# A fused attention and squared-ReLU kernel: the opening is laid out by other costs, three chunks of the first expanded weights go by DMA, and s is applied at the eviction

## The chip, the cores and the metric

The kernel runs on one core of a Trainium2 chip. The metric is the device time of one execution in microseconds (us). The text calls TensorE PE, VectorE DVE, ScalarE ACT, GpSimd POOL and SyncE SP, as the profile does. SP only issues DMAs here.

## What is computed

There are B = 4 batches of N = 12480 rows x of C = 128 columns, m = 32 inducing rows, and d_ff = 2048. Everything is float32.

```python
scale = 1.0 / np.sqrt(C)
def mab(q, kv):
    s = scale * (q @ kv.transpose(0, 2, 1))
    s = s - s.max(-1, keepdims=True)
    a = np.exp(s)
    a /= a.sum(-1, keepdims=True) + 1e-09
    return a @ kv
h = mab(I, x)
attn = mab(x, h)
...
h = attn @ w_in
r = np.maximum(h, 0.0)
g = s * (r * r) + b
return g @ w_out
```

The weights w_in, w_out and the scalars s and b are float64 in DRAM; the kernel narrows the weights to float32 itself.

## The kernel before

A batch has 26 blocks of 480 rows. Before the first block of a batch, all its rows attend to the inducing rows, which gives h (32 x 128), kept transposed as `hT`. Then `attend` gives the weights of each row on the 32 rows of h (`a2t`, transposed, with high and low halves so that fp32r products keep float32 precision). The second `@ h` and `@ w_in` are one product: `wst` holds h @ w_in (32 x 2048), four times below one another as high and low halves. So a block needs eight *pairs* (`pair`): two matmuls mm1 (L1002, 128x480 each) into a PSUM tile h, a ReLU r (L1014 on ACT or L1016 on DVE), the square's high half (L1080, ACT), the low half (L1045 on DVE, then L1056 on POOL or DVE, or by a DMA that adds), and six matmuls by `w_hi` and `w_lo` (L1112, `out_part`) into one of two PSUM banks x. The bank leaves with the bias by L1125 and a DMA. Work on the next blocks and the next batch stands between the pairs. 4 x 26 x 8 = 832 pairs make the steady stage.

The first batch has no batch ahead of it to hide in: this is the **opening**. The first batch's x comes in 13 tiles of 960 rows (480 KB; x0 to x12). Each tile is scored against the inducing rows (`first_scores`, L568, groups of one or two tiles), and its transposed copy is made by PE and a copy (`turn_x`, L542, L284) or loaded by DMA (`load_first`, L515). The eight chunks of float64 weights (512 KB each: i0 to i3 of w_in, o0 to o3 of w_out) are narrowed (`narrow`, L427 to L445): two masks on DVE, two ACT steps, two DVE steps, and one product on POOL (or DVE). A chunk of w_out is then split into `w_hi` (ACT, L455) and `w_lo` (DVE, L457), both scaled by s; `w_neg` (L464) is two pieces of -w_hi. When the last tile, x0, is scored, the maxima and sums are joined (`h_unit`, `h_sums`, `h_out`: L617 to L690) to `hT`. `attend_first` (L903 to L942) makes the first block's a2t alone; `w_unit` (L703 to L707) makes the four chunks of wst. Then pair 0 can begin.

The order on each engine isn't that of the code. A planner (`Plan.run`) takes units of work with a cost in us, an engine or a choice of them, events that they wait for, and an urgency; it picks what can start soonest, shifted by urgency times a weight, and writes the instructions in that order. `LOCK` marks a DVE step that the planner doesn't place beside a POOL step. `Rules` are its weights, one set for the opening and one for every 32 pairs. Its times only set the order: on the chip each engine runs its list in order, and each instruction waits for what it needs.

```python
yield "ACT", 0.6, ("w_out", c)
nc.scalar.mul(w_hi[:, sl, :], raw[:, sl, :], s_sb)
yield "DVE", 0.63, LOCK
nc.vector.scalar_tensor_tensor(
    out=w_lo[:, sl, :], in0=raw[:, sl, :], scalar=s_sb, in1=w_hi[:, sl, :].bitcast(F32),
    op0=ALU.mult, op1=ALU.subtract,
)
```

In the profile buffer numbers are left out: g stands for g, g1 (raw weights, high halves of squares) and g2, x for the two PSUM banks, h for the PSUM tiles, s for several small tiles. wst is the name of the expanded weights and, in the opening, of the narrowed w_out.

## Time and profile before

| | before |
|---|---|
| median of 3 runs | 1520.68 us (1519.18 to 1521.63) |
| the profiled execution's own time | 1518.01 us |
| its span, first to last instruction | 1516.2 us |
| busy: PE, DVE, ACT, POOL | 99%, 95%, 97%, 95% |
| PE's granted clock | 0.999 |
| first ReLU of pair 0 begins | 53.73 us |
| last eviction ends, last instruction | 1511.93 us, 1516.2 us |

The profile is of one execution. Times are from the start of its span. Most work of PE is in L1112 and L1002; their matmuls overlap, so that a mean of 367 ns for one stands beside a start every 0.20 us. A row of the timeline gives start, duration, engine, line, operation, output and inputs, and in brackets how long the engine had been idle and what ended that.

### The profile page before, as it was taken

The numbers are of one execution on the slowest core, as the hardware profiler recorded it, in microseconds if no ns is written. First come the engines' busy times: TensorE is split into PE (matmuls) and PEld (weight loads), VectorE is DVE, ScalarE is ACT, GpSimd is POOL, SyncE is SP. The second block draws the span as 40 slices with busy tenths as digits, with TensorE's granted clock in tenths as the row PEclk, the third lists the DMA queues.
The fourth block names the chain that finished last, engine by engine and source line by source line (L and its number), as shares of the span: only waits on it lengthen the run. The fifth ranks groups of instructions, "written<-read, shape, count | busy, mean of one in ns | idle before, by whom it ended". The sixth has DMA issues, their size and how long they took to land.

```text
span 1516.2 us, 25236 instructions
## 1 busy us (share of the span) xinstructions
PE 1495.3 (99%) x8215; PEld 1294.9 (85%) x8215; DVE 1435.3 (95%) x1587; ACT 1465.4 (97%) x1767; POOL 1443.7 (95%) x725
## 2 busy tenths in 40 slices
PE   7899999999999999999999999999999999999998
PEld 5588888888888888888898888888889888888887
DVE  5899999999999999999999999999999999999998
ACT  6899999999999999999999999999999999999997
POOL 2599999999999999999999999999999999999998
PEclk9999999999999999999999999999999999999999
DMA  9244545534454454453455534544533334234332
GB/s 342 65 124 128 140 104 158 143 76 125 104 150 127 114 149 105 135 142 83 127 133 137 144 104 118 163 112 105 120 102 93 79 91 112 56 85 108 91 72 53
DMA packets 73810, 178.91 MB, mean 118 GB/s; under 512 B 13520, under 2 KB 40144, under 8 KB 73680
## 3 DMA queue, kind: packets, MB, share of 16 engines
q1 hardware_dynamic: 59280, 128.51, 27.2%
q0 software_dynamic: 14256, 48.67, 17.3%
q8 instruction: 67, 1.10, 0.3%
q14 instruction: 63, 0.52, 0.1%
q10 hardware_dynamic: 144, 0.12, 0.0%
HBM read 74.56 MB, written 25.56 MB: 66 GB/s over the span
## 4 chain that ended last, share of the span: by engine, by line
PE 69%; ACT 4%; issue 3%; POOL 3%; DVE 2%; DVEq 0%; ACTq 0%; POOLq 0%
PE x L1112 48%; PE h L1002 17%; POOL g L1056 3%; ACT r L1014 2%; ACT g L1080 2%; PE x L853 1%; DVE g L1045 1%; PE x L802 1%; PE x L762 1%; DVE h L1045 0%; DVE r L1016 0%; DVE gm L1027 0%; PE x L717 0%; ACT ob L1125 0%; POOL hm L1032 0%
## 5 line engine op out<-in xcount | busy, mean ns | idle before, releaser
L1056 POOL TENSOR_TENSOR g<-g,g 128x960 fp32r<-128x960 f32 x611 | 1399.2, 2665 | 21.7 <-DVE g L1045 13.4
L1112 PE MATMUL x<-g,w_hi 128*128 128x480 f32 x2932 | 920.1, 367 | 1.5 <-POOL g L1056 1.0
L1080 ACT ACTIVATE g<-r 128x960 fp32r<-128x960 f32 x733 | 713.4, 1008 | 12.0 <-PE x L1112 0.9
L1045 DVE SCALAR_TENSOR_TENSOR g<-h,r 128x960 f32<-128x960 f32 x611 | 688.5, 1146 | 24.2 <-ACT r L1014 13.7
L1014 ACT ACTIVATE r<-h 128x960 f32<-128x960 f32 x648 | 608.6, 970 | 12.5 <-PE h L1002 10.2
L1112 PEld LDWEIGHTS x<-g,w_hi 128*128 128x128 f32 x2932 | 550.8, 189 | 52.5 <-issue 6.3
L1112 PE MATMUL x<-g,w_lo 128*128 128x480 f32 x1466 | 537.4, 367 | 1.4 <-ACT g L1080 1.1
L1002 PE MATMUL h<-a2t,wst 128*128 128x480 f32 x1664 | 485.4, 374 | 3.7 <-DVE g L1045 3.2
L1002 PEld LDWEIGHTS h<-a2t,wst 128*128 128x128 f32 x1664 | 299.2, 189 | 82.2 <-issue 33.1
L1112 PEld LDWEIGHTS x<-g,w_lo 128*128 128x128 f32 x1466 | 277.0, 189 | 24.5 <-issue 2.6
L1016 DVE TENSOR_SCALAR r<-h 128x960 f32<-128x960 f32 x184 | 210.8, 1148 | 5.0 <-PE h L1002 3.8
L1056 DVE TENSOR_TENSOR g<-h,g 128x960 fp32r<-128x960 f32 x122 | 140.7, 1153 | 7.8 <-ACT g L1080 1.2
L1045 DVE SCALAR_TENSOR_TENSOR h<-h,r 128x960 f32<-128x960 f32 x122 | 141.0, 1155 | 0.9 <-ACT r L1014 0.8
L1027 DVE SCALAR_TENSOR_TENSOR gm<-h,r 128x960 f32<-128x960 f32 x99 | 113.3, 1145 | 4.3 <-ACT r L1014 4.1
L1032 POOL DMA_DIRECT2D hm<-gm x99 | 113.7, 1148 | 0.1
L1080 ACT ACTIVATE hm<-r 128x960 fp32r<-128x960 f32 x99 | 99.7, 1007 | 0.7
L1112 PE MATMUL x<-hm,w_lo 128*128 128x480 f32 x198 | 72.8, 368 | 0.0
L1112 PE MATMUL x<-hm,w_hi 128*128 128x480 f32 x198 | 72.5, 366 | 0.0
L1125 ACT ACTIVATE ob<-x,bias 128x480 f32<-128x480 f32 x101 | 66.8, 661 | 1.1 <-PE x L1112 0.5
L1112 PE MATMUL x<-hm,w_neg 128*128 128x480 f32 x198 | 56.3, 366 | 0.0
L1112 PEld LDWEIGHTS x<-hm,w_lo 128*128 128x128 f32 x198 | 37.4, 189 | 3.5 <-DVE hl L891 0.8
L1112 PEld LDWEIGHTS x<-hm,w_neg 128*128 128x128 f32 x198 | 37.4, 189 | 2.7
(152 smaller groups left out, 559.4 us busy)
## 6 DMA issues: line engine op xcount, KB each, us to landing
hm<-gm POOLq DMA_DIRECT2D x99, 480.0 KB, 5.3
xt<-in_xT_dram SPq DMA_DIRECT2D x96, 480.0 KB, 5.2
a2t<-hl SPq DMA_DIRECT2D x412, 60.0 KB, 2.0
out_dram<-ob SPq DMA_DIRECT2D x103, 240.0 KB, 2.1
xn<-in_xN_dram SPq DMA_DIRECT2D x18, 512.0 KB, 4.3
xn<-in_xN_dram SPq DMA_DIRECT2D x18, 448.0 KB, 4.8
wst<-whl SPq DMA_DIRECT2D x48, 64.0 KB, 2.0
g<-in_w_in_dram SPq DMA_DIRECT2D x4, 512.0 KB, 10.3
```

Source lines behind the costliest of these rows:

```text
L762: nc.tensor.matmul(ps[M * q:M * (q + 1), 0:BLK], ind_sb, xt[:, q % SB], start=True, stop=True)
L802: nc.tensor.matmul(ps[M * c:M * (c + 1), 0:P], eT[0:rows, n], xn_tiles[b, g, half][0][0:rows, n - half * TH], start=n < P // M, stop=n + P ...
L1002: nc.tensor.matmul(h[:, u, 0:BLK], wst[:, n * P:(n + 1) * P], by_turns(A), start=True, stop=True)
L1014: nc.scalar.activation(out=r, in_=hv, func=AF.Relu)
L1016: nc.vector.tensor_scalar(out=r, in0=hv, scalar1=0.0, scalar2=None, op0=ALU.max)
L1027: nc.vector.scalar_tensor_tensor(out=gm, in0=hv, scalar=-1.0, in1=r, op0=ALU.mult, op1=ALU.mult)
L1032: nc.gpsimd.dma_start(out=hi["t"].bitcast(F32).rearrange("p u t -> p (u t)"), in_=gm.rearrange("p u t -> p (u t)"), accum_op=ALU.add,)
L1045: nc.vector.scalar_tensor_tensor(out=g, in0=hv, scalar=0.0, in1=r, op0=ALU.max, op1=ALU.mult)
L1056: eng.tensor_tensor(out=g2, in0=g, in1=hi["t"].bitcast(F32), op=ALU.subtract)
L1080: nc.scalar.activation(out=hi["t"], in_=r, func=AF.Square)
L1112: nc.tensor.matmul(o, w, by_turns(g), start=first and n == 0, stop=left == 0 and n == len(ops) - 1)
L1125: nc.scalar.activation(out=ob, in_=o, func=AF.Identity, bias=bias, scale=1.0)
```

## The change

The opening's loads, until now written by tile with weights between them, follow a list `ORDER`: x2, x3, the inducing rows, x5, x7, x9, x6, x10, then weights among the other tiles; b and s come late, and three chunks of w_out behind x0. The groups of tiles are others, and three transposed tiles come by DMA (x8, x9, x11) instead of two (x5, x9). The planner's costs for the opening are others: what an issue on SP takes, when each engine begins, when a load lands, a PE that takes double after a pause. Urgencies are given by chunk. `w_unit` makes chunk 0 of wst alone; the other three are made as in later batches (`w_tiles`, `w_spread`): one PSUM bank, one ACT copy, one DVE subtraction, and twelve DMAs on SP. `w_hi` is a plain copy and `w_lo` a plain subtraction that may go to POOL; s is applied where a block leaves, with the bias. The last block leaves in one ACT step and one DMA on ACT's queue, not in two halves on two engines. The steady stage's `Rules` are others in most of the 26 rows.

```diff
-W_IN_U = -100
...
-FIRST_GROUPS = ((2, 3), (4, 5), (6, 7), (8, 9), (10, 11), (12, 1), (0,))
-BY_DMA = [5, 9]
-W_AFTER = [1, 2, 6, 8, 1, 5, 7, 12]
-WARM = 6
...
+FIRST_GROUPS = ((2, 3), (5, 10), (4, 12), (7, 11), (9, 8), (6, 1), (0,))
+
+ORDER = [
+    "x2", "x3", "ind", "x5", "x7", "x9", "x6", "x10", "i0", "i2", "x12", "x4", "i1", "x8", "x11",
+    "f11", "x1", "i3", "f8", "f9", "o1", "b", "s", "x0", "o0", "o2", "o3",
+]
+WARM = 4
+ISSUE = 0.46
+BEGIN = {"SP": 0.74, "PE": 1.8, "ACT": 2.0, "DVE": 2.3, "Pool": 2.2}
+COLD = 4.9
...
-OPENING = Rules(0.0229, 0.0865, -0.624, 0.022, -8.4567, 5.0037, 2.0571, -1.5635, -15.3862, 2.8109, 2.7863, -1.9358, 2.4761, 1, 1)
+OPENING = Rules(0.0029, 0.0909, -2.3408, 0.1198, -34.9628, 5.8368, 7.8162, 11.7675, -103.0989, -1.3642, -1.9256, -5.1828, 7.8315, 1, 1)
...
-            self.start, self.end = at, at + u[3][self.eng] + IDLE * idle
+            if self.eng == "PE" and at - self.free.get("PE", 0.0) > PAUSE:
+                self.since = at
+            cold = self.eng == "PE" and self.rules is OPENING and at < self.since + COLD
+            self.start, self.end = at, at + u[3][self.eng] * (1 + cold) + IDLE * idle
...
         yield "ACT", 0.6, ("w_out", c)
-        nc.scalar.mul(w_hi[:, sl, :], raw[:, sl, :], s_sb)
-        yield "DVE", 0.63, LOCK
-        nc.vector.scalar_tensor_tensor(
-            out=w_lo[:, sl, :], in0=raw[:, sl, :], scalar=s_sb, in1=w_hi[:, sl, :].bitcast(F32),
-            op0=ALU.mult, op1=ALU.subtract,
+        nc.scalar.copy(out=w_hi[:, sl, :], in_=raw[:, sl, :])
+        yield dict(DVE=0.63, Pool=1.5), W_LEAN, LOCK
+        (nc.gpsimd if plan.eng == "Pool" else nc.vector).tensor_tensor(
+            out=w_lo[:, sl, :], in0=raw[:, sl, :], in1=w_hi[:, sl, :].bitcast(F32), op=ALU.subtract
         )
...
-        for c in range(F // WC):
+        for c in range(0 if b else 1, F // WC):
             plan.spawn(w_spread(b, c, whl, wst), SPREAD, plan.end + LAT)
...
-        if blk_g == B * NBLK - 1:
-            for half, eng in ((0, "ACT"), (1, "DVE")):
-                plan.spawn(last_half(o, c0, half, eng), 0.0, plan.end + LAT)
-            return
-        yield dict(ACT=0.54, DVE=0.58), 0.0, "bias"
+        last = blk_g == B * NBLK - 1
+        yield dict(ACT=0.54) if last else dict(ACT=0.54, DVE=0.58), 0.0, "bias"
         ob = p2.tile([P, BLK], F32, name="ob")
         if plan.eng == "ACT":
-            nc.scalar.activation(out=ob, in_=o, func=AF.Identity, bias=bias, scale=1.0)
+            nc.scalar.activation(out=ob, in_=o, func=AF.Identity, bias=bias, scale=s_sb)
         else:
-            nc.vector.tensor_scalar(out=ob, in0=o, scalar1=bias, scalar2=None, op0=ALU.add)
-        nc.sync.dma_start(out=outT[:, c0:c0 + BLK], in_=ob)
+            nc.vector.tensor_scalar(out=ob, in0=o, scalar1=s_sb, scalar2=bias, op0=ALU.mult, op1=ALU.add)
+        (nc.scalar if last else nc.sync).dma_start(out=outT[:, c0:c0 + BLK], in_=ob)
...
-        for c in range(F // WC):
-            if c == F // WC - 1:
-                plan.spawn(with_spare(keep_warm), FIRST + 190.0)
-            plan.spawn(with_spare(w_unit, 0, c), FIRST + W_URGENCY[c])
-        plan.spawn(attend_first(), FIRST + 1.0)
+        plan.spawn(with_spare(w_unit, 0, 0), FIRST + W_URGENCY[0])
+        plan.spawn(with_spare(w_tiles, 0), FIRST + W_URGENCY[1])
+        plan.spawn(with_slot(keep_warm_slot), FIRST + 190.0)
+        plan.spawn(attend_first(), FIRST + FIRST_U["attend"])
```

How the instructions stand now is shown at three places. In these rows a number behind a name is that of the buffer.

The first DMAs of the program on SP; xt, gm, hm and g are homes of tiles of x, g1 holds raw weights. Before:

```order
L374 DMA xt_120<-in_xT_dram 128x960
L1221 DMA ind_sb_87<-in_indT_dram 128x32
L1222 DMA s_sb_88<-in_s_rep_dram 128x1
L1223 DMA b_sb_89<-in_b_rep_dram 128x1
L386 DMA gm_126<-in_xT_dram 128x960
L412 DMA g1_132<-in_w_in_dram 128x1024
L412 DMA g1_135<-in_w_out_dram 128x1024
L386 DMA hm_137<-in_xT_dram 128x960
L412 DMA g1_140<-in_w_in_dram 128x1024
L386 DMA gm_142<-in_xT_dram 128x960
```

Now:

```order
L401 DMA hm_120<-in_xT_dram 128x960
L401 DMA hm_122<-in_xT_dram 128x960
L1236 DMA ind_sb_87<-in_indT_dram 128x32
L388 DMA xt_130<-in_xT_dram 128x960
L388 DMA xt_133<-in_xT_dram 128x960
L388 DMA xt_137<-in_xT_dram 128x960
L401 DMA g_139<-in_xT_dram 128x960
L388 DMA xt_141<-in_xT_dram 128x960
L427 DMA g1_144<-in_w_in_dram 128x1024
L427 DMA g1_151<-in_w_in_dram 128x1024
```

Seven tiles of x now stand ahead of the first chunk of weights, where one more tile did. Up to x0 there are 22 large loads before (13 of x, 2 transposed, 7 of weights) and 21 now (13, 3, 5).

The first block's attention on DVE, behind the subtraction of the maxima (L909, now L931) and up to the low half hl (L931, now L957); g2 are steps of narrowing, h and x_86 PSUM. Before:

```order
L442 SCALAR_TENSOR_TENSOR wst<-g_332,wst 128x512
L913 MEMSET s_675 120x4
L916 TENSOR_REDUCE l_679<-s_675 120x4
L918 RECIPROCAL l_679<-l_679 120x4
L921 TENSOR_TENSOR s_675<-s_675,l_679 120x4x32
L707 TENSOR_TENSOR wst<-h,wst 64x512
L931 TENSOR_TENSOR hl<-s_675,hl 120x8x32
```

Now:

```order
L453 SCALAR_TENSOR_TENSOR g_614<-g_536,g_614 128x512
L936 MEMSET s_646 120x4
L442 TENSOR_SCALAR g_651<-g_555 128x512
L457 SCALAR_TENSOR_TENSOR wst<-g_536,wst 128x512
L446 TENSOR_SCALAR g_658<-g_555 128x512
L939 TENSOR_REDUCE l_662<-s_646 120x4
L942 RECIPROCAL l_662<-l_662 120x4
L946 TENSOR_TENSOR s_646<-s_646,l_662 120x4x32
L720 TENSOR_TENSOR wst<-h,wst 64x512
L446 TENSOR_SCALAR g_675<-g_546 128x512
L453 SCALAR_TENSOR_TENSOR g_651<-g_555,g_651 128x512
L957 TENSOR_TENSOR hl<-s_646,hl 120x8x32
```

Six steps of narrowing o0, o2 and o3 stand in that chain where one stood.

The same stretch on ACT, from the exponential (L912, now L935) to the first a2t (L942, now L969). Before:

```order
L912 ACTIVATE s_675<-x_86 120x4x32
L705 CAST wst<-h 128x512 x2
L929 CAST hl<-s_675 120x8x32
L705 CAST wst<-h 128x512 x2
L942 CAST a2t<-x_86 128x480
```

Now:

```order
L935 ACTIVATE s_646<-x_86 120x4x32
L470 CAST w_hi<-wst 128x512
L718 CAST wst<-h 128x512
L448 ACTIVATE g_651<-g_651,floor 128x512
L450 ACTIVATE wst<-g_658 128x512
L470 CAST w_hi<-wst 128x512
L955 CAST hl<-s_646 120x8x32
L448 ACTIVATE g_631<-g_631,floor 128x512
L737 CAST whl<-h 128x512
L450 ACTIVATE wst<-g_675 128x512
L478 ACTIVATE w_neg<-w_hi 128x256 x2
L969 CAST a2t<-x_86 128x480
```

Eleven instructions stand between the exponential and a2t where five did. POOL's list ahead of its first product of a pair (L1056, now L1084) held the eight products of narrowing; now it holds these and three of the four w_lo, and the fourth stands behind that first product.

## Rows read from the trace of the kernel before

**Rows 1.** Busy time by stretch: us, PE, PEld, DVE, ACT, POOL, clock, DMA share, GB/s

```profile
100.00:200.00 100.00, 100.00 (x534) 85.69 (x533) 95.54 (x105) 99.02 (x117) 99.92 (x51) 1.00 0.49 127
...
60.00:1510.00 1450.00, 1445.66 (x7699) 1262.65 (x7699) 1397.60 (x1501) 1421.53 (x1680) 1428.35 (x709) 1.00 0.44 113
```

**Rows 2.** The same view, an early stretch of the opening

```profile
2.00:4.00 2.00, 2.00 (x5) 1.55 (x6) 0.00 (x0) 0.02 (x1) 0.11 (x1) 1.00 0.76 228
```

**Rows 3.** Timeline, SP: the issues of x3 and of x0

```profile
2.59 0.43 SPq L386 DMA_DIRECT2D gm<-in_xT_dram  x1
...
25.07 0.33 SPq L374 DMA_DIRECT2D xt<-in_xT_dram  x1
```

**Rows 4.** From issue to landing, one load each: x2 (issued 0.74), x3, x0

```profile
DMA to landing us min/median/max: 3.4/3.4/3.4
...
DMA to landing us min/median/max: 4.7/4.7/4.7
...
DMA to landing us min/median/max: 9.7/9.7/9.7
```

**Rows 5.** Timeline, DVE, behind the last scores: the joined maximum, and hT

```profile
39.92 0.28 DVE L620 TENSOR_REDUCE mrow<-h 1x32 f32<-1x128 f32 x1 [1.39 <-PE h L617]
...
45.24 0.29 DVE L690 COPY hT<-h 128x128 f32<-128x128 f32 x1 [0.85 <-PE h L687]
```

**Rows 6.** Timeline, from the first block's exponential to the first ReLUs

```profile
47.42 0.28 ACT L912 ACTIVATE s<-x 120x128 f32<-120x128 f32 x1 [2.06 <-DVE x L909]
...
49.44 0.41 ACT L929 CAST hl<-s 120x256 fp32r<-120x256 f32 x1
...
51.45 0.56 ACT L942 CAST a2t<-x 128x480 fp32r<-128x480 f32 x1 [0.45 <-PE x L934]
...
52.08 1.01 PE L853 MATMUL x<-xt,hT 128*32 128x480 f32 x8
...
53.73 1.83 ACT L1014 ACTIVATE r<-h 128x960 f32<-128x960 f32 x2 [1.10 <-PE h L1002]
```

**Rows 7.** Groups by line, first 62 us: busy us, mean ns | idle before

```profile
L433 ACT ACTIVATE g<-g,floor 128x512 int32<-128x512 int32 x8 | 5.6, 729 | 0.0
...
L455 ACT ACTIVATE w_hi<-wst,s_sb 128x512 fp32r<-128x512 f32 x4 | 2.9, 720 | 0.0
...
L435 ACT ACTIVATE wst<-g 128x512 f32<-128x512 int32 x4 | 2.4, 626 | 0.0
L705 ACT CAST wst<-h 128x512 fp32r<-128x512 f32 x4 | 2.2, 586 | 0.8 <-PE h L703 0.7
...
L464 ACT ACTIVATE w_neg<-w_hi 128x256 fp32r<-128x256 f32 x2 | 0.7, 428 | 0.0
...
L457 DVE SCALAR_TENSOR_TENSOR w_lo<-wst,s_sb,w_hi 128x512 fp32r<-128x512 f32 x4 | 3.5, 870 | 0.6 <-ACT w_hi L455 0.6
...
L445 POOL TENSOR_TENSOR wst<-wst,g 128x512 f32<-128x512 f32 x4 | 5.2, 1309 | 28.0 <-DVE wst L442 24.4 <-DVE s L913 3.6
```

**Rows 8.** Timeline: DVE and POOL with operands in SBUF at one time

```profile
30.25 1.38 POOL L445 TENSOR_TENSOR w_in_sb<-w_in_sb,g 128x512 f32<-128x512 f32 x1 [0.74 <-DVE w_in_sb L442]
30.42 1.50 DVE L431 TENSOR_SCALAR g<-g 128x512 int32<-128x512 int32 x1
31.84 0.42 DVE L427 TENSOR_SCALAR g<-g 128x512 int32<-128x512 int32 x1
...
48.57 0.83 DVE L921 TENSOR_TENSOR s<-s,l 120x128 f32<-120x128 f32 x1
```

**Rows 9.** Timeline: the two halves of the last eviction

```profile
1510.97 0.46 ACT L1095 ACTIVATE ob<-x,bias 128x240 f32<-128x240 f32 x1 [4.03 <-PE x L1112]
...
1511.46 0.47 DVE L1097 TENSOR_SCALAR ob<-x,bias 128x240 f32<-128x240 f32 x1 [2.07 <-ACT ob L1095]
```

**Rows 10.** Output DMAs: count, KB each, median us to landing; all, and the last

```profile
out_dram<-ob SPq DMA_DIRECT2D x103, 240.0 KB, 2.1
...
out_dram<-ob SPq DMA_DIRECT2D x1, 120.0 KB, 1.7
```

More of the change, by code (lines that the diff above doesn't have):

```diff
@@ L358, in tile_attn_relu2 @@
     raws = {}
-    dma = [2.7]
+    dma = [0.0]
     def landing(us):
-        dma[0] = max(dma[0], plan.end + 3.0) + us
-        if dma[0] < 5.0:
-            dma[0], us = 6.2, dma[0]
-            return us
+        if ("mm1", 0) not in plan.events:
+            dma[0] = max(dma[0], plan.end + FIRST_LAND)
+            dma[0] += us * (SLOW if dma[0] < 7.0 else 1.0)
+        else:
+            dma[0] = max(dma[0], plan.end + 3.0) + us
         return dma[0]
@@ L492, in tile_attn_relu2 @@
     home = {j: ("r", "xn")[n] for js in FIRST_GROUPS for n, j in enumerate(js)}
-    turned = [j for j in order if j not in BY_DMA]
+    by_dma = [int(n[1:]) for n in ORDER if n[0] == "f"]
+    turned = [j for j in order if j not in by_dma]
     def x_used(j):
@@ L505, in used @@
                 plan.set(("x", 0, j, 2))
-        left = [2]
+        left = [1 if j in by_dma else 2]
         return used
     def load_first(j):
-        n, free = ring_in_order("xn", 2)
-        yield "SP", 0.05, *free
-        t = xn_pool.tile([P, SB, NQ, P], F32, name="xn", bufs=2)
-        plan.set(("xn", "got", n))
+        yield "SP", ISSUE, room("g1", G1)
+        n = take("g1")
+        t = ew.tile([P, SB, NQ, P], F32, name="g1", bufs=G1)
         nc.sync.dma_start(out=t.rearrange("p a q c -> p (a q c)"), in_=xF[j])
-        xn_tiles[0, j] = [(t[0:T, a], ("xn", n)) for a in range(SB)]
+        xn_tiles[0, j] = [(t[0:T, a], ("g1", n)) for a in range(SB)]
         plan.events["xn", 0, j] = landing(1.3)
@@ L562, in first_scores @@
         d = st[0]
-        yield "PE", 0.45 * len(js), *[("x", 0, j, 1) for j in js], *waits
+        yield "PE", 0.45 * len(js), "ind", *[("x", 0, j, 1) for j in js], *waits
         s, turned_e = ps()
@@ L697, in w_unit @@
         sl = slice(c * WC, (c + 1) * WC)
-        yield "PE", 0.85, ("hT", b), ("w_in", c), *waits
-        if c == 0:
-            d["wst"] = wst_pool.tile([P, F], F32R, name="wst")
+        yield "PE", 0.94, "asked", ("w_in", c), *waits
+        d["wst"] = wst_pool.tile([P, F], F32R, name="wst")
         wst = d["wst"]
@@ L712, in w_tiles @@
         d = st[b]
-        yield "PE", 1.19, ("hT", b), *[("w_in", c) for c in range(F // WC)], *waits
-        wst = d["wst"] = wst_pool.tile([P, F], F32R, name="wst")
+        yield "PE", 1.19, ("hT", b), *[("w_in", c) for c in range(F // WC)], *([] if b else [("wst", 0, 0)]), *waits
+        if b:
+            d["wst"] = wst_pool.tile([P, F], F32R, name="wst")
+        wst = d["wst"]
         ps = ps()
@@ L895, in attend, with hold @@
             plan.spawn(spread(b, g, q), SPREAD, plan.end + LAT)
+    def hold(**engines):
+        for eng, us in engines.items():
+            plan.free[eng] = max(plan.free.get(eng, 0.0), plan.end + us)
     def attend_first():
-        yield "PE", 1.0, ("hT", 0), ("x", 0, 0, 2)
+        yield "PE", 0.93, ("hT", 0), ("x", 0, 0, 2)
         ps, hT = bank[1], st[0]["hT"]
@@ L922, in attend_first @@
         n, free = ring_in_order("hl", 2)
-        yield "ACT", 0.28, *free
+        hold(DVE=HOLD[2])
+        yield "ACT", 0.3, *free
         hl = p2.tile([P, 2, BLK], F32R, name="hl")
@@ L929, in attend_first @@
         nc.scalar.copy(out=hi, in_=both)
-        yield "DVE", 0.33
+        yield "DVE", 0.3
         nc.vector.tensor_tensor(out=lo, in0=both, in1=hi.bitcast(F32), op=ALU.subtract)
-        yield "PE", 0.3
+        hold(ACT=HOLD[3])
+        yield "PE", 0.4
         for q in range(NQ):
@@ L945, in attend_first @@
         plan.set("first")
+        yield "SP", 0.0, ("mm1", 1)
         front_work(0)
@@ L1260, in keep_warm @@
     def keep_warm(ps, *waits):
-        while plan.events.get(("a2t", 0, 0), math.inf) > plan.end + 0.3:
+        for _ in range(90):
+            if plan.events.get(("a2t", 0, 0), math.inf) <= plan.end + 0.3:
+                break
             yield from warm(1, ps, *waits)
```

152 lines of the change are left out of this document (82 added, 70 removed).

## Prediction

> **What bounds the kernel now.** I read the busy time by stretch first, then the timeline of the opening, the issues and landings of its loads, and last the groups of lines for durations. The steady stage is bound by PE: between 60 and 1510 us it is idle for 1450.00 - 1445.66 = 4.3 us, while DVE, ACT and POOL have 52, 28 and 22 us to spare [rows 1]. The number of matmuls doesn't change, so what the change can win there is at most those 4.3 us. What is left is the time before PE gets its first pairs. Pair 0's first ReLU begins at 53.73 [rows 6]; whatever moves that and the filling of the pipeline behind it moves the end, as PE then hardly stops.
>
> The opening before is a chain of three pieces. The last tile of x, x0, is issued at 25.07 and lands 9.7 later, at 34.8 [rows 3, 4]. From there to hT at 45.53 [rows 5] is 10.7 us. From hT to the first a2t, at 51.45 + 0.56 = 52.0 [rows 6], is 6.5 us; then comes 1.0 us of PE's work for the next blocks (L853), and mm1 of pair 0.
>
> **The change, part by part.**
>
> *Loads.* x3 lands at 2.59 + 4.7 = 7.3 [rows 3, 4]. The 20 large loads from there to x0 take 34.8 - 7.3 = 27.5 us, 1.37 each, with the DMA queue never empty. Now x2 and x3 stand first. x2 lands at 0.74 + 3.4 = 4.1 [rows 4]. x3 adds one tile, 0.49 MB: 2.2 us at the early 228 GB/s [rows 2], 1.37 at the mean. I take 1.6, nearer the mean because two loads now overlap: 5.7. Then 19 loads come up to x0: 5.7 + 26.1 = 31.8. **Gain 3.0**; it is 1.4 if the early start is worth nothing and one load less is all, 3.3 with x3 at the mean price. SP's list waits for buffers: o1, and x0 behind it, wait until i2 is narrowed. i2 is the seventh load behind x3 (5.7 + 7 x 1.37 = 15.3), and its six steps of 0.4 to 1.3 are done by about 20; the queue then still holds five loads or more, so no DMA idles. o0, o2 and o3 wait until i1 is narrowed, behind x0's scores, at about 35. By the 3.4 of a lone load [rows 4] the first lands at about 38.4 and the others 1.37 apart; their masks are due on DVE from 40 to 45, so they are just in time. If they are late, the first block's chain stands behind them on DVE.
>
> *From x0 to hT.* Before, DVE stood idle 1.39 us for the joined maximum [rows 5], because PE's products ahead of it waited for ACT, which was behind by then. Now ACT has fewer copies (one more transposed tile comes by DMA, three chunks of w_out come after x0). The rest is a chain of small steps that stays, and DVE gets three steps of narrowing between them, mostly where it would wait. I take **0.3** of gain, between 0 and 1.4. hT then stands at 42.2, which is 3.3 earlier.
>
> *From hT to a2t.* Here the order loses. Before, ACT has 51.45 - 47.70 = 3.75 us from the end of the exponential to the cast of a2t [rows 6]. Now eleven instructions stand between: two each of 0.72 (as L455), 0.59 (L705), 0.73 (L433), 0.63 (L435) and 0.43 (L464), and the 0.41 of the high half: 6.6 by durations [rows 6, 7]. Two in a row take less than their sum: two ReLUs of 0.97 were 1.83 [rows 6]; with 0.11 off for each it is 5.4. **Loss 1.6** against 3.75; bounds 1.3 (a plain copy for w_hi at 0.59) and 2.8 (nothing overlaps). DVE's own list for this stretch, six steps of narrowing longer, is about as long, so that here no cover is left: what holds DVE now holds a2t. I add **0.5**, the one hold that the chain had before (a product took 0.83, [rows 8], on the tile for which ACT takes 0.28, [rows 6]).
>
> *mm1 ahead of the next blocks.* Before, mm1 stood behind L853, 1.01 us [rows 6]; now two pairs' mm1 come first. The ReLU of pair 0 follows a2t by 0.8 instead of 53.73 - 52.01 = 1.7: **gain 0.9**. The third and fourth pair need chunk 1 of wst, which now comes by four DMAs behind DVE's step for whl, but these pairs have room: ACT turns to them only after two ReLUs (1.83), a w_hi and a square.
>
> *Behind the first ReLU.* ACT has two w_hi left where it had one: **loss 0.6** by L455 less the overlap. DVE loses two w_lo of 0.87 [rows 7] and gets one step of narrowing more: -1.0. POOL gets two w_lo and one product of narrowing more, 1.3 each by L445 [rows 7]: +3.9. POOL had 28.0 us of idle time ahead of such products in the opening, little of it behind the first ReLU. I set DVE and POOL against each other: 0, between -1.0 and +1.5.
>
> *s at the eviction.* 104 evictions read s as well. L455, which reads s, takes 0.13 more than L705, which reads nothing beside its input [rows 7]; at most 104 x 0.13 = 14 us of ACT, beside 28 us that ACT is idle in the steady stage [rows 1]. On the path: 0. If ACT's room were not where it is needed, up to 14 us would show.
>
> *The last eviction.* The DVE half began when the ACT half had ended [rows 9]. One eviction of 480 columns ends about 0.3 sooner; its DMA has twice the bytes, and lands in 2.1 where the half took 1.7 [rows 10]. Sum 0, bounds -0.3 and +0.4.
>
> *The planner's cold PE and its rules.* The doubled cost of a PE that has paused and four warm-up products for six only set the order; the granted clock is 1.00 early and late [rows 1, 2], and nothing is set down for it. The steady rules reorder pairs; best case -4.3 (all idle time of PE gone), and as much lost in the worst. Two lists made by the same rules are likely to be alike: 0.
>
> *Sum*: -3.0 - 0.3 + 1.6 + 0.5 - 0.9 + 0.6 = **-1.5 us**. The profiled execution took 1518.01 for a span of 1516.2, so it would become 1516.5; it stood 2.67 under the median of 1520.68, which becomes **1519.2**. A measurement of this kernel tells about 0.2% (3.0 us) from no change.
>
> **A row against the change.** A mask on DVE took 1.50 us while a POOL product ran from 30.25 to 31.63; the like one behind it took 0.42 [rows 8]. So a DVE step whose operands are all in SBUF can stand until POOL's has ended. Four POOL steps of 1.3 now fall between hT and the end of the first block's DVE chain (two products of narrowing, two w_lo), where one did. The sum above has one hold of 0.5. The Trainium skill (SBUF — State Buffer, Who interferes with whom) says that a DVE instruction with two SBUF inputs, or in a two-port mode, and a GpSimd instruction that reads SBUF exclude each other for a whole instruction, whichever starts first. The trace agrees with it (1.50 against 0.42). By that rule alone, with POOL always first, the sum would be that of the last rival below; by the one row of the chain it is mine.
>
> **The rivals.**
>
> *More is gained.* ACT is no longer behind, so the whole 1.39 before the joined maximum goes (-1.1 more); no hold falls on the chain (-0.5); POOL's new work fits its idle time, and DVE's -1.0 counts. -1.5 - 2.6 = -4.1: 1516.6. For it: POOL's 28.0 us of idle time. Against it: POOL's list comes late, when DVE has made its inputs.
>
> *The gain is given back to POOL.* In the first steady stretch POOL is busy 99.92 of 100 us [rows 1], more than ACT and DVE; there it is as near a bound as PE. If its 3.9 us more behind the first ReLU, less DVE's 1.0, are shared by these two, either of which can make a pair's low half, (3.9 - 1.0) / 2 = 1.5 reaches PE: 1520.7, no change. For it: 99.92. Against it: the order may send more low halves to DVE.
>
> *The holds decide: slower.* Each of the four POOL steps holds a DVE step of the chain for its full 1.3: 5.2 in place of the 0.5. -1.5 - 0.5 + 5.2 = +3.2: 1523.9. It costs the whole gain from 2.0 us of holds on and shows as slower from 5.0 on, so nearly all four must fall first and in full. For it: DVE's list has six such steps there, and no cover. Against it: POOL's inputs come from the same DVE list, which then runs on to steps that read PSUM.
>
> **How the numbers follow.** My forecast, 1519.2 (1517.7 to 1520.2 by itself): 0.43. More gained, 1516.6: 0.28. Given back, 1520.7: 0.20. Holds, 1523.9: 0.09. Faster by over 0.2% (under 1517.6) is the second case and a corner of the first: 0.32. Slower by over 0.2% (above 1523.7) is the last: 0.09. The rest, 0.59, is within. The range begins 1.8 below the second case, for the loads' bound (0.3) and part of the steady rules' 4.3, and ends at 1522.5, 1.8 above the third, for the unknowns on the other side: 1514.8 to 1522.5.
>
> **What would show it.** In the profile after: x0's landing near 31.8; hT near 42; the cast of a2t, now behind eleven ACT instructions, at about 50.5 to 51, and the first ReLU within 1 us of it; masks and two-operand steps on DVE longer than 0.42 and 0.7 while POOL runs; PE idle for 4 to 5 us between 60 and 1510. I am wrong if x0 lands after 33.5, if the first ReLU begins before 50 or after 54, if DVE waits for o0, o2 or o3 to land ahead of hT's chain, if the mm1 of the third pair waits long for the spread DMAs, or if PE's idle time in the steady stage changes by more than 1.5 us.

## The result and the profile after

The change makes the kernel slower. Its median is 1529.87 us (1528.84 to 1531.29, 4 runs), that of the kernel before on the same chip 1520.85 us; the ratio is 1.0061, 95% interval 1.0044 to 1.0079. A second measurement on another chip gave 1530.64 us and 1.0071 (1.0058 to 1.0083). The profiled execution took 1529.86 us for a span of 1528.1 us, against a span of 1516.2 us before: 11.9 us more.

First the busy time by stretch, as in [rows 1]: two stretches of the opening in which the clock fell, the handover to the pairs, and the steady stage (columns: us, PE, PEld, DVE, ACT, POOL, clock, DMA share, GB/s).

```profile
16.00:18.00 2.00, 0.00 (x0) 0.00 (x0) 1.83 (x5) 1.54 (x4) 0.00 (x0) 1.00 1.04 419
20.00:22.00 2.00, 2.00 (x11) 1.73 (x9) 1.94 (x5) 1.17 (x2) 0.45 (x2) 0.50 1.02 415
50.00:52.00 2.00, 0.76 (x2) 0.16 (x2) 2.00 (x3) 1.73 (x4) 1.30 (x1) 1.00 0.07 16
52.00:54.00 2.00, 1.76 (x7) 1.16 (x8) 1.97 (x4) 0.56 (x1) 0.41 (x1) 0.99 0.22 49
54.00:56.00 2.00, 2.00 (x6) 1.52 (x5) 0.11 (x1) 0.00 (x0) 1.27 (x1) 0.50 0.44 99
56.00:58.00 2.00, 2.00 (x11) 0.60 (x10) 0.63 (x1) 1.63 (x2) 0.00 (x0) 0.66 0.48 109
60.00:1510.00 1450.00, 1440.58 (x7656) 1255.88 (x7656) 1393.82 (x1497) 1418.12 (x1670) 1428.44 (x711) 1.00 0.45 114
1200.00:1300.00 100.00, 97.67 (x476) 86.88 (x475) 94.58 (x96) 96.46 (x112) 97.15 (x50) 1.00 0.38 92
```

In the steady stage PE is now idle 1450.00 - 1440.58 = 9.4 us, 4.3 before [rows 1]; 2.3 of it lies between 1200 and 1300 us. In the opening the granted clock stands at 0.50, the lower of the two levels (1.2 GHz), twice: behind a stretch in which PE did nothing (16 to 18), and behind one in which it worked 0.76 of 2 us (50 to 52). The profiled execution before has 1.00 throughout its opening, though PE worked only 0.50 us there from 54 to 56: such a fall doesn't come in every execution, as the last section shows.

The timeline of the change from hT to the first ReLU, where [rows 5, 6] had hT at 45.24, the cast of a2t at 51.45 and the ReLU at 53.73:

```profile
42.70 0.29 DVE L704 COPY hT<-h 128x128 f32<-128x128 f32 x1 [0.51 <-PE h L701]
...
48.60 2.70 POOL L472 TENSOR_TENSOR w_lo<-wst,w_hi 128x512 fp32r<-128x512 f32 x2 [0.73 <-ACT w_hi L470]
48.78 1.38 DVE L446 TENSOR_SCALAR g<-g 128x512 int32<-128x512 int32 x1
...
50.08 1.77 DVE L453 SCALAR_TENSOR_TENSOR g<-g,g 128x512 int32<-128x512 int32 x1
...
51.77 0.41 DVE L957 TENSOR_TENSOR hl<-s,hl 120x256 fp32r<-120x256 f32 x1
...
52.24 0.66 PE L961 MATMUL x<-ident_r,hl 120*128 120x120 f32 x4 [1.48 <-DVE hl L957]
...
52.73 2.79 PE L1283 MATMUL h<-hl 128*128 128x480 f32 x6
...
52.94 0.56 ACT L969 CAST a2t<-x 128x480 fp32r<-128x480 f32 x1 [1.21 <-PE x L961]
...
55.35 1.38 PE L1030 MATMUL h<-a2t,wst 128*128 128x480 f32 x3
56.37 0.97 ACT L1042 ACTIVATE r<-h 128x960 f32<-128x960 f32 x1 [2.87 <-PE h L1030]
```

hT is 2.5 us earlier than before, but a2t is ready at 53.50, 1.5 later, and the ReLU 2.6 later. ScalarE's eleven instructions ahead of the cast of a2t are done at 51.73, 1.21 before it, so they aren't what a2t waits for. It waits for the low halves hl, the last step of a list on VectorE that has no gap longer than 0.4 us; two of its steps, a mask and a two-operand step, take 1.38 and 1.77 us beside POOL's w_lo, where the like ones elsewhere take 0.42 and 0.69. And behind a2t the first mm1 doesn't follow at once: six keep-warm products (L1283: products with no use but to keep PE at work) stand ahead of it on PE and take 2.79 us, one every 0.43 us, where in e3 below eight of them stand 0.22 apart. The first three start before the rows show the clock fall at 54; why they are slow already, no run tells. mm1 starts 1.85 us after a2t.

To see where the rest is lost I cut each trace at two places that every version has: the end of hT, and the issue of the output of block 16 (the 17th block, just past 300 us). The third stretch runs to the issue of the last block's output. Executions of one list of instructions differ by up to 2 us in when hT comes (41.4 to 43.3 us in the change, e4, e5 and e6), so the second and third columns are what can be compared. The second still holds a part that is the clock's: in e9, for one, the clock was 0.50 from 56 to 58, and before it wasn't.

```
kernel            hT ends   hT to block 16   block 16 to the last
before              45.5        260.8             1205.1
the change          43.0        267.1             1213.4
difference          -2.5         +6.3               +8.3
```

So in this execution the opening gives back all that an earlier hT won and 3.8 us more, and the larger part of the loss comes in the steady stage, most of it in its last quarter (block 80 is 5.4 us late, block 84 10.2, block 96 9.0, the last 12.1).

### The profile page after: what moved, and what is told of

Its sections match the earlier page's. It is cut to its first block, busy times and chain, and to the rows that moved or that the text cites. A ratio compares the mean times of both kernels' runs of the same rounds, so it can differ in the third digit from the quotient of the medians.

```text
span 1528.1 us, 25317 instructions
## 1 busy us (share of the span) xinstructions
PE 1503.4 (98%) x8227; PEld 1300.0 (85%) x8227; DVE 1439.5 (94%) x1587; ACT 1463.8 (96%) x1753; POOL 1454.7 (95%) x732
## 5 line engine op out<-in xcount | busy, mean ns | idle before, releaser
L1084 POOL TENSOR_TENSOR g<-g,g 128x960 fp32r<-128x960 f32 x613 | 1401.8, 2642 | 20.5 <-DVE g L1073 10.7
L1073 DVE SCALAR_TENSOR_TENSOR g<-h,r 128x960 f32<-128x960 f32 x613 | 690.2, 1147 | 25.0 <-ACT r L1042 16.5
L1030 PEld LDWEIGHTS h<-a2t,wst 128*128 128x128 f32 x1664 | 299.5, 189 | 86.5 <-issue 31.8
L1044 DVE TENSOR_SCALAR r<-h 128x960 f32<-128x960 f32 x191 | 219.1, 1149 | 5.4 <-PE h L1030 3.0
L1084 DVE TENSOR_TENSOR g<-h,g 128x960 fp32r<-128x960 f32 x119 | 137.3, 1154 | 10.3 <-ACT g L1108 3.4
L1073 DVE SCALAR_TENSOR_TENSOR h<-h,r 128x960 f32<-128x960 f32 x119 | 137.6, 1157 | 2.2 <-ACT r L1042 1.8
L1139 ACT ACTIVATE ob<-x,bias,s_sb 128x480 f32<-128x480 f32 x104 | 78.2, 752 | 5.7 <-PE x L1129 5.3
## 6 DMA issues: line engine op xcount, KB each, us to landing
g<-in_w_in_dram SPq DMA_DIRECT2D x4, 512.0 KB, 10.4
```

What stands on the lines that cost most here:

```text
L1030: nc.tensor.matmul(h[:, u, 0:BLK], wst[:, n * P:(n + 1) * P], by_turns(A), start=True, stop=True)
L1044: nc.vector.tensor_scalar(out=r, in0=hv, scalar1=0.0, scalar2=None, op0=ALU.max)
L1073: nc.vector.scalar_tensor_tensor(out=g, in0=hv, scalar=0.0, in1=r, op0=ALU.max, op1=ALU.mult)
L1084: eng.tensor_tensor(out=g2, in0=g, in1=hi["t"].bitcast(F32), op=ALU.subtract)
L1139: nc.scalar.activation(out=ob, in_=o, func=AF.Identity, bias=bias, scale=s_sb)
```

## The experiments

The same three columns for all runs, with the ratio to the kernel before on the chip of each:

```
run                                  ratio (95%)               hT    hT-b16   b16-last
e5  the change again                 1.0071 (1.0058-1.0083)   43.3    267.1    1214.1
e1  the change, old steady table     1.0151 (1.0137-1.0165)   41.6    267.5    1223.4
e2  before, new steady table         1.0035 (1.0022-1.0047)   45.6    261.6    1209.9
e3  the change, wait filled          1.0066 (1.0052-1.0080)   42.3    265.0    1214.1
e4  the change, no factor s          1.0056 (1.0044-1.0069)   42.7    266.4    1212.3
e6  the change, order of before      1.0032 (1.0021-1.0042)   41.4    267.1    1208.6
e7  e6, wait filled                  1.0027 (1.0018-1.0036)   42.4    265.0    1208.5
e8  e7, s folded, w_lo on VectorE    1.0020 (1.0011-1.0029)   41.5    267.4    1206.1
e9  before, s at the eviction        1.0025 (1.0016-1.0034)   44.5    261.9    1208.3
e10 e7, no factor s                  1.0004 (0.9995-1.0013)   43.4    264.4    1205.9
e11 e6, six products left out        1.0030 (1.0019-1.0041)   42.2    265.5    1208.8
e12 four w_units for the spread      1.0058 (1.0044-1.0071)   44.2    270.2    1207.6
e13 e11, w_lo on VectorE             1.0039 (1.0024-1.0053)   41.1    269.8    1207.7
e14 e8, two products for eight       1.0018 (1.0004-1.0031)   44.9    269.3    1205.7
```

**The theories.** One: the opening is late because PE's clock falls and the six keep-warm products stand ahead of the first mm1. Rivals for the opening: POOL's w_lo hold VectorE, or the weights spread by DMA come late. For the steady stage: the order that the new table sets is worse on the chip, or the factor s at the eviction costs, or an opening that comes late costs more and more whatever the order.

**The steady tables, exchanged (e1, e2).** e1 is the change with the table of before, e2 the reverse; no other line differs.

```diff
-STEADY = [ 26 rows of the change ]
+STEADY = [ 26 rows of the kernel before ]
```

(The rows themselves are left out, here and below.)

> The changed kernel with the steady table of the kernel before; the opening (the first 16 pairs) stays that of the change, instruction for instruction. Theory 'the new steady table costs': block 0 still leaves at about 81.9 us and the lateness stays near +4 to 5 us to the end, without the +7 us that the change gathers after block 80; total about 1523. Theory 'any table that was fitted to another opening pays': the old table meets an opening it was not fitted to as well, and the total stays at 1526 to 1533, with waits of TensorE that move to other places. Theory 'the scale at the eviction costs': nothing moves, 1530.

> The kernel before with the new steady table alone. Theory 'the new steady table costs': the opening stays at 77.0 us for block 0 and about +7 us appear by the end, about 1528, most of them after block 80. Theory 'any table that was fitted to another opening pays': some loss too, 1523 to 1528, but at other blocks than in the change. Theory 'the scale at the eviction costs': the tables are alike, 1521 within 1.

Both are slower than the kernel whose opening they have: e1 by 0.8 to 0.9% than the change, with intervals that don't touch, e2 by 0.35% than before, with an interval wholly above 1. So neither table is the better one behind both openings. That is the direction of the second theory, but neither run fits it in full: e1 lost more than it allowed (1542 against 1526 to 1533), and e2, whose 1524.4 is in its range, loses at the blocks of the change, where it had other blocks. PE from 60 to 1510 us, e1 and e2 (columns as above):

```profile
60.00:1510.00 1450.00, 1436.14 (x7610) 1244.46 (x7611) 1381.15 (x1487) 1420.54 (x1669) 1396.67 (x695) 1.00 0.44 113
```

```profile
60.00:1510.00 1450.00, 1442.97 (x7675) 1259.23 (x7674) 1395.60 (x1497) 1417.88 (x1676) 1428.19 (x709) 1.00 0.44 113
```

PE stands idle 13.9 and 7.0 us there, where [rows 1] had 4.3. By the names of their tiles, the last 6442 of some 8220 products on PE are the same in e2 and in the change; and e2 loses at the same place (block 80 is 0.9 us late, block 84 5.7: 4.8 between them, as in the change), so this part needs neither the new opening nor s.

**The order of before behind the opening of the change (e6), beside the change (e5).** With four rows of the new table and 22 of the old, the planner falls back into the order of the kernel before: from block 19 on PE's list is the same, product for product.

```diff
-STEADY = [ new rows 0 to 25 ]
+STEADY = [ new rows 0 to 3, old rows 4 to 25 ]
```

> The changed kernel itself, on the chip of the next three: 1.005 to 1.008 of the kernel before. Block 0 leaves at 81.9 us, block 16 about 3.8 late, block 103 about 12 late.

> The changed kernel with the new steady table's first four rows and the other 22 rows of the old table: from block 19 on, TensorE's order is then the order of the kernel before, product for product, behind the opening of the change. Theory 'the order that the new rows set from block 19 on costs 5 us, the opening 4': the lateness stays at +3 to +5 us from block 20 to block 103, without the steps at blocks 81 to 97, and the ratio is 1.002 to 1.004 (about 1525). Theory 'a late opening costs more the longer it runs, whatever the order': +9 to +12 at block 103 again, ratio 1.005 to 1.008. Theory 'the scale at the eviction costs in the steady part': +2 to +4 grow in evenly over the blocks, ratio 1.004 to 1.005.

1.0071 becomes 1.0032 on one chip: the new order costs 0.0039 of 1519, **5.9 us**, and by the traces 1214.1 - 1208.6 = 5.5. The steps at block 84 are gone. PE is idle 1450.00 - 1445.43 = 4.6 us:

```profile
60.00:1510.00 1450.00, 1445.43 (x7683) 1258.17 (x7683) 1397.62 (x1502) 1425.16 (x1677) 1428.09 (x710) 1.00 0.45 114
```

So the order is it, and the theory that a late opening by itself costs more and more falls. (e12 and e13, much later than e6 at block 16, need less time from there.) But the lateness still grows by 3.4 us from block 16 to the last, bit by bit. The ratio is that of the first theory, the even growth is what the third set down for s at the eviction; PE's idle time, 4.6 us against 4.3, doesn't show it.

What the new order does at the worst of these places, the timeline of the change:

```profile
1212.00 1.17 DVE L1073 SCALAR_TENSOR_TENSOR h<-h,r 128x960 f32<-128x960 f32 x1
...
1213.08 1.15 DVE L1073 SCALAR_TENSOR_TENSOR g<-h,r 128x960 f32<-128x960 f32 x1
...
1214.14 1.15 DVE L1084 TENSOR_TENSOR g<-h,g 128x960 fp32r<-128x960 f32 x1
1215.37 0.64 PE L1030 MATMUL h<-a2t,wst 128*128 128x480 f32 x2 [1.76 <-DVE g L1084]
```

A pair whose product stays in its bank h (L1073 h<-h) keeps the bank until its low half (L1084) is made. Here VectorE does another pair's product between the two, and the next mm1, which needs the bank, waits 1.76 us. At 1436.79 the wait is another (1.72 us, DMA a2t<-hl): SP's list had an output, which waits for ScalarE's eviction, ahead of the spread of a2t. The first wait stands in e2 too, behind the opening of before:

```profile
1210.94 0.64 PE L1002 MATMUL h<-a2t,wst 128*128 128x480 f32 x2 [1.82 <-DVE g L1056]
```

Between 70 and 1505 us PE has no gap over 0.9 us before and in e6; the change and e5 have these two, e2 the first. What each costs alone is read from the trace; no kernel was run that takes one of them away.

**s at the eviction (e4, e9, e10).** e9 is the kernel before with s moved and nothing else; e10 is e7 and e4 is the change, both with the factor left out.

```diff
-        nc.scalar.mul(w_hi[:, sl, :], raw[:, sl, :], s_sb)
+        nc.scalar.copy(out=w_hi[:, sl, :], in_=raw[:, sl, :])
...
-    nc.scalar.activation(out=ob, in_=o, func=AF.Identity, bias=bias, scale=1.0)
+    nc.scalar.activation(out=ob, in_=o, func=AF.Identity, bias=bias, scale=s_sb)
```

> The kernel before with s moved to the evictions alone: w_hi is a copy, w_lo one subtraction on VectorE, each eviction multiplies by s; every instruction stands where it stood. Theory 's at the eviction costs the steady part': ScalarE's evictions go from 0.66 to 0.68 up to 0.74 to 0.79, the lateness grows evenly with the blocks to +2.4 to +3.5 us at block 103, ratio 1.0015 to 1.0025. Rival 'what grew in the seventh run was the order of blocks 0 to 18, or w_lo on POOL': ratio 1.000 within 0.0007.

> The seventh run (the opening of the change with the wait filled, the steady order of before) without the factor s at the evictions: the output lacks the factor s; w_lo stays on POOL. Theory 's at the eviction costs the steady part': block 16 about +1.1, block 103 +1.1 to +2, ratio 1.0005 to 1.0012 where the seventh run had 1.0027. Rival 'the gain of the eighth run came from w_lo on VectorE': +4 at block 103 again, ratio 1.0025 to 1.003.

> The changed kernel with its evictions without the factor s (scale 1.0 on ScalarE, the bias alone on VectorE): the output lacks the factor s. Nothing else moves. Theory 'the scale at the eviction costs': each eviction on ScalarE falls from 0.74 to 0.79 back to 0.66 to 0.68, about 0.08 x 103 = 8 us of ScalarE, and if these bind the total falls to 1521 to 1524. Rival 'ScalarE has room at the evictions': 1530 within 0.8.

e9 makes the kernel before 0.25% slower, **3.8 us**, and every instruction of PE, POOL and SP stands where it stood. e10 against e7 is 1.0004 against 1.0027: 3.5 us (they ran on two chips, each beside the kernel before). By the traces it is less, 3.2 and 2.6 us from block 16 to the last. The groups of ScalarE's eviction in e9 and in e10 (busy us, mean ns | idle before):

```profile
L1122 ACT ACTIVATE ob<-x,bias,s_sb 128x480 f32<-128x480 f32 x101 | 76.2, 754 | 0.8 <-PE x L1109 0.5
```

```profile
L1142 ACT ACTIVATE ob<-x,bias 128x480 f32<-128x480 f32 x102 | 67.5, 662 | 5.4 <-PE x L1132 4.9
```

The eviction takes 754 ns with the scale read from a tile and 662 without: 92 more. The Trainium skill (ScalarE: Activation LUTs, What ACT_TABLE_LOAD costs) gives about 93 ns for each operand of one value per partition that an instruction points to; the trace agrees. 101 of the evictions make 9.3 us of ScalarE, and three to four tenths of that reach the end, spread over the blocks. (The lateness of e9 against before is 0 at block 16, 1.2 at 48, 3.2 at 103.) PE's idle time doesn't show this loss: 1450.00 - 1446.15 = 3.9 us in e9, 4.3 before. The theories of e9 and e10 hold, with e10 just under its range. e4 was a miss as an experiment: in the order of the change the missing factor moved the time by no more than its interval, and 1527.0 lies between its theory and its rival. Its execution has PE at work for only 2.89 of the 5 us from 1210, and the clock falls behind it:

```profile
1210.00:1215.00 5.00, 2.89 (x13) 2.31 (x12) 2.92 (x3) 3.19 (x4) 5.00 (x4) 0.90 0.69 148
1215.00:1220.00 5.00, 5.00 (x21) 4.45 (x20) 2.63 (x3) 3.19 (x4) 2.19 (x2) 0.76 0.09 23
```

**Clock and keep-warm products (e3, e7, e11).**

```diff
         yield "PE", 0.4
+        for _ in range(8):
+            nc.tensor.matmul(ps[:, 0:BLK], warm_sb[:, 0:P], warm_sb[:, 0:BLK], start=True, stop=True)
+        enough[0] = True
...
-            nc.tensor.matmul(ps()[:, 0:BLK], warm_sb[:, 0:P], x, start=True, stop=True)
+            if not enough[0]:
+                nc.tensor.matmul(ps()[:, 0:BLK], warm_sb[:, 0:P], x, start=True, stop=True)
```

e11 has no loop of eight; e7 is this on e6.

> The changed kernel with the wait for the last halves filled: eight keep-warm products ahead of the four that turn the first asked block (where TensorE stood idle from 50.17 to 52.24 us), and none of the six behind them, ahead of the first mm1. Theory 'the clock and the six products make the opening late': the granted clock stays at 1.00 from 50 to 58 us, the first mm1 starts about 53.7 instead of 55.35, the first ReLU about 54.5 instead of 56.37, block 0 leaves at 80 instead of 81.9, and the total is 1527.5 to 1528.5. Rival 'the holds and the spread weights bind behind it': the first ReLU comes earlier, but block 0 leaves at 81.5 or later and the total is 1530 within 0.7.

> The last one and, as in e3, eight keep-warm products ahead of the four that turn the first asked block and none of the six behind them. Theory 'clock and queue of keep-warm products make the opening late': block 16 about 2.8 us earlier than in the last run, kept to the end: ratio 1.000 to 1.002. Rival 'a gain in the opening is taken back by later waits': the same ratio as the last run within 0.0008.

> The sixth run without the six keep-warm products ahead of the first mm1, and with nothing in the wait before them. Theory 'the queue of six is most of it': the first mm1 follows the first asked block's halves by 0.6 us instead of 2.4, though the granted clock still falls to 0.50 soon after; block 16 is 1 us earlier than in the sixth run. Theory 'the clock is most of it': mm1 follows by 0.6 us, but the products behind it run at half clock until after 56 us or longer, since TensorE is now idle longer, and block 16 is as late as in the sixth run or later.

e3, the timeline, and the busy time by stretch:

```profile
52.27 0.56 ACT L972 CAST a2t<-x 128x480 fp32r<-128x480 f32 x1 [1.22 <-PE x L964]
...
52.88 1.08 PE L1033 MATMUL h<-a2t,wst 128*128 128x480 f32 x4 [0.65 <-ACT a2t L972]
...
53.59 1.83 ACT L1045 ACTIVATE r<-h 128x960 f32<-128x960 f32 x2 [0.76 <-PE h L1033]
```

```profile
52.00:54.00 2.00, 1.35 (x11) 0.89 (x13) 1.44 (x3) 0.97 (x2) 1.08 (x1) 1.00 0.17 40
54.00:56.00 2.00, 1.73 (x11) 0.54 (x10) 1.41 (x2) 2.00 (x4) 0.58 (x1) 1.00 0.46 105
```

The clock stays at 1.00, mm1 follows a2t by 0.05 us, and from hT to block 16 there are 265.0 us instead of 267.1 in both e3 and e7: **2.1 us**. (What stood idle in the change was PE from 50.76 to 52.24; the 50.17 of the expectation is the start of the product before.) e3's 1528.48 is in the range of its theory. e11 keeps the products away but leaves PE idle; mm1 follows by 0.05 us too, then the clock falls all the same,

```profile
52.00:54.00 2.00, 1.35 (x5) 0.82 (x4) 1.31 (x3) 1.02 (x2) 1.21 (x1) 0.80 0.19 43
54.00:56.00 2.00, 2.00 (x10) 0.21 (x9) 1.46 (x2) 2.00 (x4) 0.48 (x2) 0.50 0.46 107
```

and 265.5 are left: 1.6 of the 2.1 is the queue of six, 0.5 the clock behind it. In the medians less shows (1.0032, 1.0030, 1.0027 for e6, e11, e7: 0.8 us from first to last, inside the intervals), and e3's 1.0066 can't be told from the change's 1.0071. By its ratio e7 would be its rival's; but from block 16 to the last e6 and e7 take 1208.6 and 1208.5, so nothing is taken back. The part shows in the traces and is small.

**POOL's w_lo and the fold (e8, e13, e14).** e13 is e11 with w_lo on VectorE; e8 and e14 have w_lo on VectorE, which multiplies by s in the same step, and the evictions of before.

```diff
-        (nc.gpsimd if plan.eng == "Pool" else nc.vector).tensor_tensor(
+        nc.vector.tensor_tensor(
             out=w_lo[:, sl, :], in0=raw[:, sl, :], in1=w_hi[:, sl, :].bitcast(F32), op=ALU.subtract
         )
```

> The last one with s in the second weights again: w_hi is s times the weights on ScalarE, w_lo is taken on VectorE in one step as in the kernel before (not on POOL), and the evictions carry the bias alone. Theory 's at the eviction costs ScalarE 0.08 us in each of some 100 blocks and POOL's w_lo holds VectorE': the first asked block's halves come about 0.9 us earlier and the steady part gains up to 2 to 4 us: ratio 0.997 to 0.999. Rival 'both lie beside other work': the ratio of the last run within 0.0008.

> The eleventh run (six keep-warm products left out, nothing in their place) with all four w_lo on VectorE in place of POOL; s stays at the evictions. Theory 'POOL's w_lo holds VectorE ahead of the first asked block': from hT to the low halves hl 7.7 us on VectorE instead of 9.1, and now nothing stands on TensorE ahead of the turning products, so that the first mm1 comes 1.4 us nearer to hT (9.5 instead of 10.85 behind its start), and block 16 is up to 1.4 us earlier; ratio 1.002 to 1.0025. Rival 'the two steps that VectorE then has itself cost later what the holds cost now': mm1 is earlier, block 16 is not, ratio 1.003 again.

> The eighth run (s folded into the second weights again, w_lo on VectorE, the steady order of before) with two keep-warm products instead of eight ahead of the turning ones: in the eighth run the halves came at 49.27 us and TensorE was still at the eight until 50.8. Theory 'the eight then stood in the way': the first mm1 comes 1.3 us nearer to hT and the ratio is 1.0005 to 1.0015, the kernel before at best reached, not beaten. Rival 'VectorE's list and the clock behind the first ReLU decide': ratio 1.002 again, with the granted clock at 0.5 to 0.75 between 55 and 62 us.

The holds are there: the mask and the two-operand step that took 1.38 and 1.77 us beside POOL take 0.43 and 0.70 in e8, where POOL is idle then, which agrees again with the rule of the Trainium skill that the prediction cites (SBUF — State Buffer, Who interferes with whom). Without POOL's w_lo, hl is ready 7.8 us after hT, in all three, instead of 9.2, and in e13 and e14 the first mm1 is 1.3 us nearer to hT. (In e8 my own eight products, sized for the longer wait, ended 1.5 us behind the halves and hid it.) But nothing of it is kept. From hT to block 16 e13 takes 269.8 us where e11 took 265.5. The two later w_lo now stand on VectorE between the first pairs and take 1.38 and 1.25 us there, beside POOL's products, where the first two took 0.67; PE has gaps, and the clock falls behind them, as e13's stretches show:

```profile
56.00:58.00 2.00, 1.08 (x4) 0.68 (x4) 1.97 (x4) 1.03 (x3) 1.81 (x1) 1.00 0.60 108
58.00:60.00 2.00, 1.53 (x5) 0.87 (x5) 1.90 (x6) 2.00 (x4) 1.77 (x1) 0.66 0.83 309
60.00:62.00 2.00, 1.90 (x4) 1.10 (x4) 2.00 (x3) 1.10 (x2) 0.44 (x1) 0.50 0.38 154
```

It stays at 0.50 up to 72. So the rival of e13 holds: mm1 is earlier and block 16 is not. What is lost seems to be the clock's: of e13's six executions the one with a mean granted clock of 0.999 took 1521.09 us, less than any of e11's, and the one with 0.993 took 1528.33. (The planner still counted the four w_lo as POOL's steps; a list that is planned with them on VectorE wasn't run.) e8 and e14 still come to 1.0020 and 1.0018, because s is out of the steady stage (1206.1 and 1205.7 us from block 16 on, near the 1205.1 of before). Both miss the ratios of their theories (0.997 to 0.999, 1.0005 to 1.0015); e8's is within 0.0008 of e7's, as its rival had it, and in e14's traced execution the clock falls at 66, not between 55 and 62.

**The spread by DMA undone (e12).**

```diff
-        plan.spawn(with_spare(w_unit, 0, 0), FIRST + W_URGENCY[0])
-        plan.spawn(with_spare(w_tiles, 0), FIRST + W_URGENCY[1])
+        for c in range(F // WC):
+            plan.spawn(with_spare(w_unit, 0, c), FIRST + W_URGENCY[c])
```

> The changed kernel's opening with all four chunks of the first expanded weights made by products, ScalarE and VectorE (four w_units, urgencies of the kernel before) in place of one chunk and the spread by DMA; three new rows of the steady table, then the old ones, which bring TensorE's order back to that of before from about block 40. Theory 'the spread by DMA takes load off the three engines': block 0 leaves 2 to 6 us later than in the sixth run, ratio 1.006 to 1.008. Rival 'the spread DMAs are what makes pairs 2 to 5 late': block 0 leaves 1 to 3 us earlier than in the sixth run, ratio 1.001 to 1.0025.

1.0058 against e6's 1.0032, and 270.2 against 267.1 us from hT to block 16: with four w_units the opening is 3 us worse. VectorE's splitting steps stand between the first pairs, and the third pair's mm1 starts 6.3 us after the first pair's; in e6 it was 2.4:

```profile
53.33 1.05 PE L1031 MATMUL h<-a2t,wst 128*128 128x480 f32 x4
...
54.32 1.30 DVE L721 TENSOR_TENSOR wst<-h,wst 64x512 fp32r<-64x512 f32 x2
...
59.63 0.67 PE L1031 MATMUL h<-a2t,wst 128*128 128x480 f32 x2
```

The clock is lower too: 0.991 to 0.995 over e12's four executions, 0.996 to 0.998 in e6. As its theory had it, block 0 leaves 3.7 us later than in e6; the ratio is just under its range. With these urgencies, those of the kernel before, the spread is a part of the change that helps this opening; four w_units with urgencies set for it weren't run.

No version that was run beats the kernel before. The nearest that has the factor s is e14, 1.0018 (its two fastest executions, with the clock at 0.999 and 1.000, took 1518.4 and 1518.8 us, where the median of before was 1519.05); even with the factor s left out, e10, the new opening only reaches it (1.0004, 0.9995 to 1.0013).

## Why the prediction was wrong

The forecast was 1519.2 us and the range ended at 1522.5. The ratios split the loss (e5 to e7 on one chip, e10 on another): 1.0071 (e5) to 1.0032 (e6) is the order, 5.9 us; to 1.0027 (e7) clock and queue, 0.8 (2.1 by the trace); to 1.0004 (e10) s, 3.5; what is left, 0.6, is an opening that gains nothing. Two of the prediction's own signs of being wrong came: the first ReLU after 54 (56.37), and PE's idle time in the steady stage changed by more than 1.5 us (5.1). By the prediction's own steps:

- *Loads.* Right: x0 lands at 31.5 (31.8 forecast), and o0, o2 and o3 landed in time.
- *From x0 to hT.* Mis-sized: 11.5 us instead of 10.4 (10.7 before), so hT is at 42.99 instead of 42.2. The joined maximum comes 5.1 us behind x0's landing, as before, so the 0.3 of gain isn't there (in e6, whose clock kept 1.00 around 21 us, it comes 3.9 behind). From it to hT are 6.4 us, 5.6 before; 0.6 of these 0.8 lie behind the step `s` (L699): the next product (L701) stands on PE behind four keep-warm products, which hold PE until 42.26, where two stood before. VectorE's narrowing ahead of L699 is about 0.3. This is read from the trace; no run takes either away.
- *From hT to a2t.* Mis-sized: 10.5 us, not 6.5 + 2.1 = 8.6. I costed ScalarE's eleven instructions and set VectorE's list beside them as "about as long". It is the longer one: hl is ready 9.2 us behind hT, 5.2 before, and ScalarE's list was done 1.21 us before the cast. 1.4 of the 4.0 are the holds by POOL's w_lo (e8, e13, e14), for which the 0.5 stood; the other 2.6 are narrowing that now lies between hT and hl. By the durations elsewhere in the trace (0.42 for a mask, 0.68 or 0.69 for a two-operand step) the six steps less the one of before make those 2.6; no run moved them away.
- *mm1 ahead of the next blocks.* The failed step of the opening. L853 did move behind, but a ReLU 0.8 behind a2t was forecast and it came 2.87 behind. Of the cold PE and the warm-ups I wrote that the granted clock "is 1.00 early and late [rows 1, 2], and nothing is set down for it". But the change opens two waits of PE, and behind each the clock was 0.50 in this execution; and the six keep-warm products that stand ahead of mm1 in the order weren't priced at all. With them gone it is 0.8 (e3, e11).
- *Behind the first ReLU.* +0.6 forecast. e3 and e7 have it at the time of before within 0.2 us, and block 16 is about 1 us late, of which s has a part. About right.
- *s at the eviction.* The mechanism was named, with an upper bound of 14 us, and the value taken was 0. It is 0.092 x 101 = 9.3 us of ScalarE and 3.5 to 3.8 at the end (2.6 to 3.2 by the traces, from block 16 on). The argument, that ScalarE is idle 28 us, was one from an average over the whole stage; it says nothing of where that time lies.
- *The last eviction.* Right: from block 102 to the end nothing is gained or lost (11.7 us late there, 11.9 at the end).
- *The planner's rules.* The step that failed by most. "Two lists made by the same rules are likely to be alike: 0", with "as much lost in the worst", 4.3. They are not alike, and 5.9 us were lost. PE's small idle time before was no sign that any list would do, it was what this one list had reached: with the very table of before, but another opening, e1 has PE idle for 13.9 us.
- *The rivals.* "The holds decide" named a true mechanism and was too dear (1.4 us, not 5.2), and taking w_lo away from POOL gained nothing. "More gained" did not come. "Given back to POOL" can't be told apart: no run gives POOL's work back with all else as it was, and PE's idle time (4.6 us behind the order of before) doesn't show every loss, as e9 tells.

## What to carry to other kernels

In a kernel whose order a planner sets from tuned numbers, an edit of the opening is also an edit of the order of everything behind it; cost it as a new list of unknown quality, and separate the two by putting the old list behind the new opening. Add per-block costs up on each engine and, where all engines are over 95% busy, let a good part of them (here three to four tenths) reach the end. And when a stage is made to start earlier, ask which list is as long as the new chain: hT came 2.5 us sooner, and VectorE's list up to hl became 4.0 us longer.
